# Attention and two MoE layers on one core: the fourth pair's v sums get a buffer of their own and load behind the pair's keys; raw weights load one slot later; slots 6 to 16 and their neighbours get a new order

## The chip, the core and the metric

The kernel runs on one NeuronCore of a Trainium2 chip. The metric is device time in microseconds of one execution, as the median of some executions. Lower is better.

## What is computed

Three layers, one behind the other; all tensors are float32.

```python
# 1. attention, q, k, v: (2, 8, 768, 64); block 32, window 16
k_sum = k.reshape(B, H, 24, 32, D).max(axis=3)      # 24 summary keys per head
v_sum = v.reshape(B, H, 24, 32, D).mean(axis=3)     # 24 summary values per head
scores = softmax over [local keys with |i - j| < 16, 24 summary keys + log(32)]
attn   = a @ [v, v_sum]
# 2. x = attn as (1536, 512);  h = x @ w_in (512, 2048);  g = elu(h);  x2 = g @ w_out
# 3. top-1 mixture of 8 experts on x2: gate by argmax and softmax, relu(x2 @ w1[e]) @ w2[e], times the gate
```

## The kernel before

The 16 heads (2 batches of 8) are taken in pairs, two heads side by side on the 128 partitions. With the 768 tokens of a batch cut into two stretches of 384, there are 16 "pairs" p = 0 to 15: p // 4 is the stretch t, p % 4 the pair of heads. Each pair is done in two units u = 2p and 2p + 1 of three query blocks. The second layer is done in two groups of 8 chunks of the hidden width (f = 0 to 7 and 8 to 15) for each of the four stretches.

The order of all work is written out by hand: one loop over slots, `for sl in range(total)`, and in each slot the instructions are recorded in the order in which every engine and every queue runs them. A slot starts one attention unit (u = sl) while there are any, and from `LAG` = 9 on also a step n = sl - 9 of the second layer.

- Slots 0 to 7 hold attention alone, with small transposes of `busy()` that keep TensorE occupied. In a slot, `pe_s` makes the scores S on TensorE, `dve_max` adds the mask and takes the row minimum on VectorE, `act_exp` is on ScalarE, `norm` scales on VectorE and GpSimd, `pe_t` transposes into T, `act_t` copies T out as pT, `pe_o` multiplies with the values into O, `act_o` copies O out. S, T and O have one PSUM buffer each.
- `prep_k(p + 1)` builds the next pair's key windows `kw` and, for t even, the summary keys. `prep_va(p + 1)` adds up the values of the next pair, read from the tile `vt`, into `va` on VectorE; `pe_va` transposes `va` at the end of the slot, ahead of the next pair's scores; `fin_va` takes the result out as `vs`.
- Loads go through SP's queue, in order. `load_vt(p + 2)` stands in the odd slot of pair p; its tile has one buffer (tag `vt`), so the load waits until `prep_va(p + 1)` has read the buffer.
- The weights of the second layer come as raw 64-bit views: `w_prefetch` loads one raw tile of 512 KB (four buffers), `w_conv` makes float32 of it by three VectorE instructions (lines 396, 400, 403), `w_split` makes the two halves that the fast matmul wants, by a ScalarE cast (L409) and a GpSimd subtraction (L410). In slots 2 to 5 one `w_prefetch` is issued at the end of each.
- Slot 8 is written out by itself: it starts the second layer (`mm1`, line 420) on the first stretch in plain float32. Slots 9 to 16 ("dense") hold one attention unit and one step of the first group; the first stretch uses the converted weights whole, without halves, so splitting (`split_next`) only has to be ready for the second stretch, from slot 17 on.
- `fin` with group 0 takes the sums of a stretch out of PSUM (line 481). `split_x0` makes the two halves of the first stretch's attention output (lines 329, 330); it is not used before the second group, but its buffer is wanted by the last stretch, in slot 26.
- From slot 18 on (p = 9) `pe_s2` starts both units of a pair in an even slot. One of them shares a PSUM buffer with a chunk's hidden values h, so it waits until `elu_max` (line 439) has read h.
- Four converted tiles of the second group are stored to memory early, in slots 23, 27, 29 and 31 (`stash`), and read back later.

The lines that the steps touch: 172 and 173 (`load_vt`), 197 (`prep_k`, the large copy), 481 (`fin`), 899 and 900 (`stash`), 946 to 951 (which weights become ready for splitting in which slot), 1006 to 1011 (start of pair 9), 1092 (`split_x0`), 1181 to 1185 (dense slot), 1202 and 1203 (`load_vt`), 1228 (`w_prefetch`).

Of the kernel before, what the change touches and what calls it, by code (L numbers as in the profile page):

```python
# [9 lines left out]
F32 = mybir.dt.float32  # L10
# [39 lines left out]
def build(tc, cap, qT, kT, vT, vP, wi, wo, wg, wgT, wx, out):  # L50
# [6 lines left out]
    with ctx:  # L57
# [111 lines left out]
        def load_vt(p):  # L169
            t, pr = divmod(p, NPAIR)  # L170
            if t % 2 == 0:
                VT[p] = apool.tile([P, S], F32, tag="vt", bufs=1, name=f"vt{p}")
                nc.sync.dma_start(VT[p], vT[t // 2, pr])

        def load_vw(p):
# [8 lines left out]
        def prep_k(p):  # L184

            t, pr = divmod(p, NPAIR)
            kt = KT[p]
            kw = apool.tile([P, QPT, KEYS], F32, tag="kw", name=f"kw{p}")
            KW[p] = kw
            if t % 2 == 0:  # L190
                KS[p] = apool.tile([P, NSUM], F32, tag=f"ks{pr}", bufs=1, name=f"ks{p}")
                nc.vector.tensor_reduce(
                    out=KS[p], in_=kt[:, WIN : WIN + S].rearrange("p (u s) -> p u s", s=BLK),
                    op=ALU.max, axis=AX.X)
            else:
                KS[p] = KS[p - NPAIR]
            (nc.vector.tensor_copy if p > PB else nc.scalar.copy)(kw[:, :, 0:QB], kt[:, 0:TT].rearrange("p (i k) -> p i k", k=QB))
            rest = nc.gpsimd.tensor_copy if t == 0 and pr else nc.scalar.copy if t == 1 else nc.vector.tensor_copy
            rest(kw[:, :, QB:WK], kt[:, QB : QB + TT].rearrange("p (i k) -> p i k", k=QB)[:, :, 0 : WK - QB])
            (nc.gpsimd if t == 0 and pr else nc.vector).tensor_copy(  # L200
                out=kw[:, :, WK:KEYS], in_=KS[p].unsqueeze(1).to_broadcast([P, QPT, NSUM]))
# [276 lines left out]
        def fin(gr, t, tb):  # L478
            if gr == 0:
                acc[t, tb] = xpool.tile([P, DM], F32, tag=f"a{t}_{tb}", name=f"a{t}_{tb}")  # L480
                nc.scalar.copy(acc[t, tb], accp[tb])
            else:
                a = acc[t, tb]
                nc.vector.tensor_tensor(a, accp[tb], a, op=ALU.add)
                i = t * BPT + tb
                nc.sync.dma_start(x2d[i * P : (i + 1) * P, :], a)
                x2[i] = a
# [408 lines left out]
        nload = [0]  # L896


        stash = [order[2 * FPG + k] for k in (3, 7, 11, 13)]
        S0 = [LAG + 2 * FPG + d for d in (-2, 2, 4, 6)]  # L900
        kept = []

        def w_stash(sl):
# [27 lines left out]
        for sl in range(total):  # L931
# [14 lines left out]
                el = (0, 0, n) if 0 < n < FPG else el if n > FPG else None  # L946
                m2 = (0, 0, n - 1) if 0 <= n - 1 < FPG else None
            cv = list(corder.get(sl, ())) if sl >= LAG else []
            if 0 < n < FPG:
                wpend.append(splits[n - 1])  # L950
            if FPG <= n < FPG + 3:
                wpend.extend(splits[2 * n - FPG - 1 : 2 * n - FPG + 1])
            if FPG + 3 <= n < 2 * FPG - 2:
                wpend.append(splits[n + 2])

            def conv_next():
# [8 lines left out]
            def split_next():  # L965
                if wpend:
                    w_split(*wpend.pop(0))
# [34 lines left out]
            if sl >= 2 * PB:  # L1002
# [3 lines left out]
                if p == PB:  # L1006
                    if even:
                        pe_o(u - 2)
                        act_o(u - 2)
                        dve_o(u - 2)  # L1010
                        fin_va(p)
                        load_vs(p)
                if even and p + 2 < NPR:
# [8 lines left out]
                        load_vw(p + 1)  # L1022
                if el:
                    elu_exp(*el[1:])

                if gr == 1 and nj:
                    rt = t - 1
# [8 lines left out]
                        step(rt)  # L1036
                if el:
                    elu_max(*el[1:])
                    if attn:
                        g_hi(*el[1:])  # L1040
                        g_lo(*el[1:], nc.gpsimd)
# [47 lines left out]
                    blk.first(0, 1)  # L1089
                    conv_expert(0, range(6, 9), pool=range(NCHUNK))  # L1090
                split_next()
                if n in (FPG + 2, FPG + 4):
                    split_x0(n - FPG - 2)
                    split_x0(n - FPG - 1)
                w_stash(sl)
                conv_next()
                if gr == 1 and f % FPG in (3, 4, 5) and t == 3:
# [66 lines left out]
            if u < NU and sl % GPP == 0:  # L1164
                if p + 2 < NPR:
                    load_k(p + 2)
            if u < NU and sl % GPP == 1 and p + 2 < NPR:
                load_q(p + 2)
            if u < NU and sl % GPP == 1 and p and p + 1 < NPR:
# [11 lines left out]
            if dense:  # L1181
                if el:
                    g_hi(*el[1:])
                    g_lo(*el[1:], nc.gpsimd)
                split_next()
                if sl % GPP and p + 1 < NPR:
                    prep_va(p + 1)
                w_conv(cv, (0,))
                if u - 2 in late:
                    dve_o(u - 2)  # L1190
                w_conv(cv, (1,))
                norm(u)
                w_conv(cv, (2,))
                for x in cv:
                    w_prefetch()
                cv = []
            if u < NU and sl % GPP == 0 and p + 1 < NPR:
                prep_k(p + 1)
            if u < NU and sl % GPP == 1 and p + 1 < NPR:
                if not dense:  # L1200
                    prep_va(p + 1)
                if p + 2 < NPR:
                    load_vt(p + 2)
            if sl < LAG and u - 2 in late:
                dve_o(u - 2)
# [19 lines left out]
            if m1:  # L1225
                mm1(*m1[1:])
            conv_next()
            if sl in (LAG - 7, LAG - 6, LAG - 5, LAG - 4):
                w_prefetch()
            if sl < LAG - 1:  # L1230
                busy(2 if sl < LAG - 3 else 4)
# [267 lines left out]
```

## Time and profile before

| | |
|---|---|
| median of 3 runs | 507.85 us (505.27 to 509.25) |
| the profiled execution | 506.81 us |
| its span on the core | 505.0 us |
| TensorE matmul busy | 473.9 us, 94% of the span |
| VectorE, ScalarE, GpSimd busy | 331.8, 266.0, 184.4 us |

The span is what the profile's instructions cover; the execution's own time is 1.8 us longer. TensorE is the engine to watch: a place where it stands still, or where its granted clock is below full, is time that the end can get back. The first 45 us differ from the rest, since attention alone is small work with many hand-overs between engines, and since the transfers of that stretch fill the DMA engines. Idle time of the other engines matters only where TensorE waits behind it.

### The profile page before, as it was taken

To read this page: it belongs to the slowest core of one execution; us is meant where nothing else is said; L and a number is where in the kernel's file an instruction comes from. 1 tells how busy PE (TensorE), PEld (TensorE's weight loads), DVE (VectorE), ACT (ScalarE), POOL (GpSimd) and SP (SyncE) were. 2 spreads that over 40 slices of the span, in tenths; PEclk is the share of its full clock that TensorE was granted. 3 is DMA by queue.
4 is the path that set the end of the run, shared out by engine and by line. 5 is a ranking of instruction groups with operands and counts; after the bars stand their busy time and mean duration, and the time that the engine had idled before them with its cause. 6 is when DMAs were issued, how large, how long until landed. Compare 5 with 4: busy or idle time off the path is not lost. (4 is left out here: it accounts for less than half of the span.)

```text
span 505.0 us, 9045 instructions
## 1 busy us (share of the span) xinstructions
PE 473.9 (94%) x2996; PEld 394.8 (78%) x2996; DVE 331.8 (66%) x886; ACT 266.0 (53%) x667; POOL 184.4 (37%) x189
## 2 busy tenths in 40 slices
PE   6799999889999999999999999999998999999792
PEld 5565555577888889999899899988867989888581
DVE  4566998678656647884259889837686854456560
ACT  4735546676666646565433333344744865466450
POOL 4311443564433326787323333213524030030440
PEclk9979999999999999999999999999999999999998
DMA  8985775324344043449210010013635876376470
GB/s 235 264 234 160 222 240 181 110 79 151 89 144 138 27 167 126 146 126 373 87 62 2 0 62 1 18 46 117 203 115 208 288 241 208 108 225 217 151 247 15
DMA packets 42178, 73.68 MB, mean 146 GB/s; under 512 B 4220, under 2 KB 18812, under 8 KB 42096
## 3 DMA queue, kind: packets, MB, share of 16 engines
q1 hardware_dynamic: 40336, 67.53, 42.5%
q0 software_dynamic: 1760, 5.19, 3.2%
q8 instruction: 34, 0.56, 0.5%
q14 instruction: 48, 0.39, 0.3%
HBM read 62.14 MB, written 9.96 MB: 143 GB/s over the span
## 5 line engine op out<-in xcount | busy, mean ns | idle before, releaser
L427 PE MATMUL h<-xT,Wi 128*128 128x384 f32 x672 | 130.3, 340 | 0.0
L472 PE MATMUL acc<-Wo,g 128*128 128x512 f32 x504 | 126.7, 395 | 0.0
L427 PEld LDWEIGHTS h<-xT,Wi 128*128 128x128 f32 x672 | 118.0, 188 | 5.8 <-issue 1.9
L452 POOL TENSOR_TENSOR g<-e,g 128x384 fp32r<-128x384 f32 x55 | 65.2, 1185 | 132.4 <-ACT g L446 132.4
L472 PEld LDWEIGHTS acc<-Wo,g 128*128 128x128 f32 x504 | 92.9, 188 | 17.4 <-POOL g L452 0.2
L439 DVE SCALAR_TENSOR_TENSOR e<-e,h 128x384 f32<-128x384 f32 x64 | 35.3, 552 | 55.9 <-ACT e L435 53.6
L434 ACT ACTIVATE e<-h 128x384 f32<-128x384 f32 x64 | 31.5, 492 | 58.5 <-PE h L427 55.4
L446 ACT CAST g<-e 128x384 fp32r<-128x384 f32 x56 | 28.8, 514 | 49.2 <-DVE e L439 49.2
L664 DVE TENSOR_TENSOR E<-rawq,E 128x512 fp32r<-128x512 f32 x70 | 47.9, 727 | 7.3 <-ACT E L654 6.0
L796 PE MATMUL bh<-xbq,E 128*128 128x256 f32 (+1 forms) x288 | 43.3, 302 | 2.4 <-issue 1.2
L281 ACT ACTIVATE sc<-sc,st 128x120 f32<-128x120 f32 x96 | 36.7, 385 | 15.8 <-DVE st L274 15.6
L289 POOL TENSOR_TENSOR sc<-sc,st 128x360 f32<-128x360 f32 x32 | 27.4, 857 | 48.2 <-DVE st L288 36.4
L796 PEld LDWEIGHTS bh<-xbq,E 128*128 128x128 f32 x288 | 41.2, 188 | 4.5 <-issue 1.6
L654 ACT CAST E<-rawq 128x512 fp32r<-128x512 f32 x75 | 42.4, 617 | 4.1 <-issue 3.0
L785 PE MATMUL y<-E,g 128*128 128x512 f32 x168 | 41.7, 393 | 0.0
L534 DVE CUSTOM_DVE_ANT_0 dot<-a,wgb 128x512 f32<-128x512 f32 x48 | 40.0, 887 | 0.0
L785 PEld LDWEIGHTS y<-E,g 128*128 128x128 f32 x168 | 30.6, 188 | 5.7
L435 ACT ACTIVATE e<-e 128x384 f32<-128x384 f32 x64 | 33.6, 526 | 2.0
L274 DVE CUSTOM_DVE_ANT_0 sc<-S,masks 128x120 f32<-128x120 f32 x96 | 21.4, 277 | 17.1 <-PE S L249 9.5
L300 ACT COPY pT<-T 120x384 f32<-120x384 f32 x32 | 15.4, 481 | 27.3 <-PE T L296 27.3
L804 DVE TENSOR_TENSOR g<-e,g 128x256 fp32r<-128x256 f32 (+1 forms) x24 | 11.3, 469 | 25.0 <-ACT g L803 24.9
L701 POOL DMA_INDIRECT out<-ys,sidx x6 | 6.3, 1050 | 48.1 <-ACT ys L700 46.6
(248 smaller groups left out, 699.1 us busy)
## 6 DMA issues: line engine op xcount, KB each, us to landing
rawq<-wx SPq DMA_DIRECT2D x88, 256.0 KB, 4.0
rawi<-wi SPq DMA_DIRECT2D x16, 512.0 KB, 7.0
rawo<-wo SPq DMA_DIRECT2D x16, 512.0 KB, 4.3
vw<-vP SPq DMA_DIRECT2D x16, 288.0 KB, 3.3
kt<-kT SPq DMA_DIRECT2D x8, 400.0 KB, 3.4
qt<-qT SPq DMA_DIRECT2D x16, 192.0 KB, 3.1
vt<-vT SPq DMA_DIRECT2D x8, 384.0 KB, 4.2
out<-xg SPq DMA_DIRECT2D x12, 256.0 KB, 4.7
```

The lines of the kernel that those rows point to most:

```text
L281: nc.scalar.activation(out=sc[:, gi], in_=sc[:, gi], func=AF.Exp, bias=st[:, 0, gi : gi + 1], scale=-1.0, accum_out=st[:, 1, gi : gi + 1])
L427: nc.tensor.matmul(HP[t, f][:, 0:TT], lhsT=w[:, s, c * P : (c + 1) * P], rhs=xT[t][:, xs, c, :], start=c == 0 and n == 0, stop=c == NCC - ...
L434: nc.scalar.activation(out=e, in_=HP[t, f][:, 0:TT], func=AF.Exp)
L435: nc.scalar.activation(out=e, in_=e, func=AF.Relu, bias=1.0, scale=-1.0)
L439: nc.vector.scalar_tensor_tensor(out=e, in0=e, scalar=-1.0, in1=h[:, 0:TT], op0=ALU.mult, op1=ALU.max)
L452: eng.tensor_tensor(g[:, 1], EP.pop((t, f)), g[:, 0].bitcast(F32), op=ALU.subtract)
L472: nc.tensor.matmul(accp[tb], lhsT=g[:, s, tb * P : (tb + 1) * P], rhs=w[:, ws], start=f % FPG == 0 and n == 0, stop=f % FPG == FPG - 1 and ...
L534: nc.vector.tensor_tensor_reduce(out=junk, in0=x2[t * BPT + tb], in1=WGB[e // 2][:, e % 2], scale=1.0, scalar=0.0, op0=ALU.mult, op1=ALU.a ...
L654: (nc.vector.tensor_copy if m in vec else nc.scalar.copy)(EW[k][m][:, 0], raw_of(k, m))
L664: (nc.gpsimd if m in pool else nc.vector).tensor_tensor(w[:, 1], raw, w[:, 0].bitcast(F32), op=ALU.subtract)
L785: nc.tensor.matmul(ys[b], lhsT=g[:, s, b * P : (b + 1) * P], rhs=w[:, ws], start=f == 0 and n == 0, stop=f == 7 and n == 2)
L796: nc.tensor.matmul(h[:, 0:nt], lhsT=EW[k][half * NCC + c][:, ws, fc * P : (fc + 1) * P], rhs=xb[:, s, c, 0:nt], start=n == 0, stop=n == 3 ...
```

## The change

1. Pair 3's values are loaded into a tile of their own (space that later holds the stretch 2 activations, tag `xT2`), and the load is issued in the even slot of pair 1, right behind pair 3's keys, not in the odd slot.
2. The four early `w_prefetch` stand in slots 3 to 6, not 2 to 5.
3. Splits: in dense slots 15 and 16 two weights are split, not one; later slots hold correspondingly fewer.
4. `fin` of the first stretch copies on VectorE, not ScalarE. The large copy of `prep_k` for pairs 10 and 11 is on ScalarE, not VectorE.
5. At the start of pair 9 (slot 18) `act_o` and `dve_o` stand later, so `fin_va` is ahead of them.
6. `split_x0` moves from slots 19 and 21 to slots 23 and 25; the stash drops its first tile (three tiles, slots 27, 29, 31), which is then loaded and converted in the second group.

```diff
@@ load_vt
             if t % 2 == 0:
-                VT[p] = apool.tile([P, S], F32, tag="vt", bufs=1, name=f"vt{p}")
+                if p == NPAIR - 1:
+                    VT[p] = xpool.tile([P, NPAIR, S], F32, tag="xT2", name=f"vt{p}")[:, 0]
+                else:
+                    VT[p] = apool.tile([P, S], F32, tag="vt", bufs=1, name=f"vt{p}")
@@ prep_k
-            (nc.vector.tensor_copy if p > PB else nc.scalar.copy)(kw[:, :, 0:QB], ...
+            (nc.vector.tensor_copy if p >= 3 * NPAIR else nc.scalar.copy)(kw[:, :, 0:QB], ...
@@ fin
-                nc.scalar.copy(acc[t, tb], accp[tb])
+                (nc.scalar.copy if t else nc.vector.tensor_copy)(acc[t, tb], accp[tb])
@@
-        stash = [order[2 * FPG + k] for k in (3, 7, 11, 13)]
-        S0 = [LAG + 2 * FPG + d for d in (-2, 2, 4, 6)]
+        stash = [order[2 * FPG + k] for k in (3, 7, 11)]
+        S0 = [LAG + 2 * FPG + d for d in (2, 4, 6)]
@@ which weights become ready for splitting
-            if 0 < n < FPG:
+            if 0 < n < FPG - 2:
                 wpend.append(splits[n - 1])
-            if FPG <= n < FPG + 3:
-                wpend.extend(splits[2 * n - FPG - 1 : 2 * n - FPG + 1])
-            if FPG + 3 <= n < 2 * FPG - 2:
+            if FPG - 2 <= n <= FPG:
+                wpend.extend(splits[2 * n - FPG + 1 : 2 * n - FPG + 3])
+            if FPG < n < 2 * FPG - 2:
                 wpend.append(splits[n + 2])
@@ slot 18
                         pe_o(u - 2)
-                        act_o(u - 2)
-                        dve_o(u - 2)
                         fin_va(p)
...
                 if el:
                     elu_exp(*el[1:])
+                if p == PB and even:
+                    act_o(u - 2)
...
                     elu_max(*el[1:])
+                    if p == PB and even:
+                        dve_o(u - 2)
@@ from slot 18 on
-                if n in (FPG + 2, FPG + 4):
-                    split_x0(n - FPG - 2)
-                    split_x0(n - FPG - 1)
+                if n in (2 * FPG - 2, 2 * FPG):
+                    split_x0(n - 2 * FPG + 2)
+                    split_x0(n - 2 * FPG + 3)
@@ slots up to 17
                     load_k(p + 2)
+                if p + 2 == NPAIR - 1:
+                    load_vt(p + 2)
...
                 split_next()
+                if n >= FPG - 2:
+                    split_next()
...
-                if p + 2 < NPR:
+                if p + 2 < NPR and p + 2 != NPAIR - 1:
                     load_vt(p + 2)
...
-            if sl in (LAG - 7, LAG - 6, LAG - 5, LAG - 4):
+            if sl in (LAG - 6, LAG - 5, LAG - 4, LAG - 3):
                 w_prefetch()
```

SP's queue in slots 2 to 5 (kt keys, qt queries, vt values for the sums, vw values, rawi and rawo raw weights; the digit is the pair or the chunk). Before:

```order
L158 DMA kt3_274<-kT 128x800
L374 DMA rawi0_295<-wi 128x1024
L167 DMA qt3_323<-qT 128x384
L180 DMA vw2_325<-vP 96x6x128
L173 DMA vt3_337<-vT 128x768
L374 DMA rawi1_342<-wi 128x1024
L225 DMA vw2_325<-vs2_372 24x6x128
L160 DMA kt4_375<-kT 128x416
L374 DMA rawi2_395<-wi 128x1024
```

The same place of SP's queue in the changed kernel (its own line numbers):

```order
L158 DMA kt3_274<-kT 128x800
L176 DMA vt3_276<-vT 128x768
L167 DMA qt3_323<-qT 128x384
L183 DMA vw2_325<-vP 96x6x128
L377 DMA rawi0_340<-wi 128x1024
L228 DMA vw2_325<-vs2_370 24x6x128
L160 DMA kt4_373<-kT 128x416
L377 DMA rawi1_393<-wi 128x1024
L167 DMA qt4_421<-qT 128x384
L183 DMA vw3_423<-vP 96x6x128
L377 DMA rawi2_438<-wi 128x1024
```

vt3 moved from fourth place behind kt3 to the first, and each raw tile moved behind the attention loads of the next slot.

GpSimd in slots 15 to 17 (sc are attention weights being scaled, Wi and Wo the low halves of split weights). Before, and then in the changed kernel:

```order
L410 TENSOR_TENSOR Wo1_1025<-T4_495,Wo1_1025 128x512
L289 TENSOR_TENSOR sc15_1015<-sc15_1015,st15_1016 128x360
L410 TENSOR_TENSOR Wi4_1081<-T6_496,Wi4_1081 128x512
L289 TENSOR_TENSOR sc16_1071<-sc16_1071,st16_1072 128x360
L410 TENSOR_TENSOR Wo2_1120<-T6_496,Wo2_1120 128x512
L289 TENSOR_TENSOR sc17_1127<-sc17_1127,st17_1128 128x360
```

```order
L413 TENSOR_TENSOR Wo1_1025<-T4_493,Wo1_1025 128x512
L413 TENSOR_TENSOR Wi4_1028<-T6_494,Wi4_1028 128x512
L292 TENSOR_TENSOR sc15_1015<-sc15_1015,st15_1016 128x360
L413 TENSOR_TENSOR Wo2_1084<-T6_494,Wo2_1084 128x512
L413 TENSOR_TENSOR Wi5_1087<-T8_495,Wi5_1087 128x512
L292 TENSOR_TENSOR sc16_1074<-sc16_1074,st16_1075 128x360
L413 TENSOR_TENSOR Wo3_1126<-T8_495,Wo3_1126 128x512
```

Two subtractions now stand back to back in slots 15 and 16.

ScalarE from slot 17 into slot 18 (a is the stretch's sum, e and g the ELU of chunk 8). Before, and then in the changed kernel:

```order
L323 CAST xT1_705<-O15_1113 128x192
L481 COPY a0_0_1146<-acc0_0_0_728 128x512
L481 COPY a0_1_1148<-acc0_0_1_729 128x512
L481 COPY a0_2_1150<-acc0_0_2_730 128x512
L409 CAST Wi5_1152<-T8_497 128x512
L300 COPY pT16_1174<-T16_1168 120x384
L323 CAST xT2_1183<-O16_1176 128x192
L220 ACTIVATE vs9_1186<-T16_1168 24x128
L434 ACTIVATE e1_0_1191<-h1_0_1155 128x384
L435 ACTIVATE e1_0_1191<-e1_0_1191 128x384
```

```order
L326 CAST xT1_705<-O15_1119 128x192
L412 CAST Wi6_1158<-T10_496 128x512
L303 COPY pT16_1180<-T16_1174 120x384
L223 ACTIVATE vs9_1189<-T16_1174 24x128
L437 ACTIVATE e1_0_1194<-h1_0_1161 128x384
L438 ACTIVATE e1_0_1194<-e1_0_1194 128x384
L326 CAST xT2_1197<-O16_1182 128x192
```

The three copies of a left this engine (they stand on VectorE, ahead of `elu_max` of chunk 8), and pT16, vs9 and the two steps of e moved forward.

## Rows read from the trace of the kernel before

**Rows 1.** Stretches: start:end, length, each engine's busy us (instructions), clock, DMA, GB/s.

```profile
25.00:30.00 5.00, 4.04 (x31) 3.07 (x32) 2.38 (x13) 1.76 (x9) 0.79 (x1) 0.56 1.09 271
30.00:35.00 5.00, 5.00 (x50) 4.05 (x50) 3.34 (x12) 2.88 (x12) 0.79 (x1) 0.75 0.80 221
220.00:230.00 10.00, 10.00 (x53) 9.21 (x52) 7.09 (x8) 6.66 (x14) 7.71 (x8) 1.00 0.74 244
```

**Rows 2.** Timeline: start, us, engine, line, instruction [idle before <-releaser], slots 5 to 8.

```profile
24.95 0.95 DVE L206 TENSOR_REDUCE va<-vt 128x24 f32<-128x768 f32 x1 [2.88 <-DMA vt<-vT]
...
25.96 0.47 PE L214 MATMUL V<-ident,va 128*120 128x128 f32 x1 [2.89 <-DVE va L206]
...
26.36 1.47 PE L260 MATMUL S<-kw,qt 64*64 64x120 f32 x12
...
31.33 1.37 PE L260 MATMUL S<-kw,qt 64*64 64x120 f32 x12
...
34.63 0.83 PE L260 MATMUL S<-kw,qt 64*64 64x120 f32 x12
```

**Rows 3.** Timeline, the same matmuls one pair earlier, in slots 4 and 5, and two small transposes.

```profile
18.06 0.83 PE L260 MATMUL S<-kw,qt 64*64 64x120 f32 x12
...
18.82 0.44 PE L864 MATMUL warm<-ident 128*128 128x128 f32 x2
...
20.38 0.83 PE L260 MATMUL S<-kw,qt 64*64 64x120 f32 x12
```

**Rows 4.** Timeline: arrivals and conversions of raw weights in slots 2 to 8.

```profile
19.65 0.35 POOL L199 COPY kw<-kt 128x192 f32<-128x192 f32 x1 [0.52 <-DMA kt<-kT]
...
29.88 0.40 DVE L396 TENSOR_SCALAR T<-rawi 128x512 uint32<-128x512 uint32 x1
...
31.51 0.69 DVE L403 SCALAR_TENSOR_TENSOR T<-rawi,T 128x512 uint32<-128x512 uint32 x1
...
36.99 0.42 DVE L396 TENSOR_SCALAR T<-rawi 128x512 uint32<-128x512 uint32 x1
...
42.91 0.83 PE L260 MATMUL S<-kw,qt 64*64 64x120 f32 x12
```

**Rows 5.** DMA from 8 to 34 us.

```profile
DMA packets 4531, 6.46 MB, mean 249 GB/s; under 512 B 329, under 2 KB 3357, under 8 KB 4526
```

**Rows 6.** Timeline, slots 14 to 16: GpSimd's subtractions beside VectorE, and TensorE's waits.

```profile
85.58 1.27 POOL L410 TENSOR_TENSOR Wo<-T,Wo 128x512 fp32r<-128x512 f32 x1 [3.72 <-ACT Wo L409]
85.64 1.75 DVE L400 SCALAR_TENSOR_TENSOR x<-rawo,x 128x512 uint32<-128x512 uint32 x1
...
88.31 2.84 PE L468 MATMUL acc<-x,e 128*128 128x512 f32 x6 [0.41 <-DVE x L403]
...
90.25 0.68 DVE L400 SCALAR_TENSOR_TENSOR x<-rawo,x 128x512 uint32<-128x512 uint32 x1
90.54 1.52 POOL L410 TENSOR_TENSOR Wi<-T,Wi 128x512 fp32r<-128x512 f32 x1 [1.63 <-ACT Wi L409]
```

**Rows 7.** Timeline, slots 17 to 22: TensorE's waits and what stands ahead of them.

```profile
96.59 1.55 ACT L481 COPY a<-acc 128x512 f32<-128x512 f32 x3
...
99.09 0.57 PE L308 MATMUL O<-pT,vw 120*64 120x64 f32 x12 [0.79 <-ACT pT L300]
...
100.42 0.52 PE L296 MATMUL T<-ident,sc 128*120 128x128 f32 x3 [0.76 <-POOL Wi L410]
...
102.03 0.83 PE L249 MATMUL S<-kw,qt 64*64 64x120 f32 x20 [0.74 <-DVE e L439]
...
113.38 0.92 PE L351 MATMUL O<-pT,vw 120*64 120x64 f32 x24 [0.63 <-DVE xT L337]
...
115.56 0.83 PE L249 MATMUL S<-kw,qt 64*64 64x120 f32 x20 [0.91 <-DVE e L439]
...
127.62 0.83 PE L249 MATMUL S<-kw,qt 64*64 64x120 f32 x20 [0.70 <-DVE e L439]
```

**Rows 8.** Timeline, VectorE at the end of slot 25.

```profile
148.12 0.55 DVE L439 SCALAR_TENSOR_TENSOR e<-e,h 128x384 f32<-128x384 f32 x1 [2.48 <-ACT e L435]
```

More of the change, by code (lines that the diff above doesn't have):

```diff
@@ L196, in prep_k @@
                 KS[p] = KS[p - NPAIR]
-            (nc.vector.tensor_copy if p > PB else nc.scalar.copy)(kw[:, :, 0:QB], kt[:, 0:TT].rearrange("p (i k) -> p i k", k=QB))
+            (nc.vector.tensor_copy if p >= 3 * NPAIR else nc.scalar.copy)(kw[:, :, 0:QB], kt[:, 0:TT].rearrange("p (i k) -> p i k", k=QB))
             rest = nc.gpsimd.tensor_copy if t == 0 and pr else nc.scalar.copy if t == 1 else nc.vector.tensor_copy
```

## The prediction

> **What bounds the kernel now.** I read first where TensorE stands still or runs below its full clock, because in most of the span it does neither: in a stretch such as 220 to 230 us it is busy for 10.00 of 10 us at a granted clock of 1.00, while VectorE has 7.09 [rows 1]. In such a stretch only less TensorE work would help. The change takes away no TensorE instruction, so its gain must come from the holes.
>
> The largest hole is in the prologue, at the end of slot 5. VectorE waits 2.88 us for the values of the fourth pair (vt3), whose sum it can start only at 24.95; TensorE, which transposes that sum next, waits 2.89 us until 25.96 [rows 2]. The price is higher than the wait. The granted clock is 0.56 in the stretch from 25 to 30 us and 0.75 from 30 to 35 [rows 1], that is, TensorE spends most of them at the lower of its two levels, 1.2 and not 2.4 GHz: the twelve matmuls of a unit's scores take 1.47 and 1.37 us in slots 6 and 7, and 0.83 in slots 4, 5 and 8 [rows 2, 3]. What it did before the fall was to stand still for those 2.89 us.
>
> The smaller holes lie in slots 15 to 22. TensorE waits 0.41 us for the conversion of a weight [rows 6]; in slots 17 and 18 it waits 0.79, 0.76 and 0.74 us for ScalarE and what hangs on it; in slots 20 and 22 it waits 0.63, 0.91 and 0.70 us for VectorE [rows 7]. From there to past 330 us I found no wait of TensorE worth naming; nothing later is tied to an absolute time, so what is saved before should reach the end.
>
> **Step 1, the prologue.** Before, vt3 stood fourth behind kt3 in SP's queue, with 992 KB (rawi0, qt3, vw2) between them, and waited for its buffer; now it is right behind kt3 and waits for no buffer. The DMA engines move 249 GB/s on the mean from 8 to 34 us [rows 5], so I take them as full and the transfers as served in order. kt3 has landed by 19.65 [rows 4]; 384 KB more take 1.6 us, so vt3 is there by about 21.2. VectorE would reach its sum at 24.95 - 2.88 = 22.07. The wait goes, with 0.9 us to spare, and TensorE starts pair 3 at 23.1 in place of 25.96.
>
> How much of the clock comes back is read from the same code one pair earlier. From the scores of slot 4 to those of slot 5 it is 2.32 us [rows 3]; slots 6 and 7 each hold four more small transposes (two take 0.44 us with their start [rows 3], so four more about 0.4), and took 4.97 and 3.30 us [rows 2]. At full clock that would be 2.7 each, so 2.9 us less in all. Not all of it arrives: VectorE converts the first raw weight in slot 6 (the three instructions take about 2.3 us, from 29.88 on [rows 4]), so the row minima of slot 7 start some 0.3 us later than TensorE would allow, and slot 8's scores need the same PSUM buffer. I take 2.5. With 2.9 for the wait, slot 8 starts 5.4 us earlier. Bounds: 2.9 if the clock falls anyway, 5.8 if nothing holds it back.
>
> What is late next? Every raw tile is issued later, but its need also comes 5.4 us earlier. The five transfers from kt3 to rawi0 are those that before went from kt3 to vt3, in another order, so rawi0 lands when vt3 did, at 24.95. It is needed 3.5 us after slot 6's scores [rows 2, 4], of which 0.6 is the slow clock, so at 26.2: 1.2 us to spare. rawi1 has 792 KB more ahead of it and in it, 3.3 us, so it lands at 28.2 and is needed in slot 7, about 30.3. rawi2 has another 992 KB, 4.1 us: 32.3, and VectorE wants it at about 32.6, where before it was 36.99 [rows 4]. That is the tightest, but TensorE uses the result only after slot 9's scores at 42.91 - 5.4 = 37.5, so a delay of up to 3 us there should stay hidden behind slot 8's matmuls. In the queue itself nothing that attention needs moves back: qt3, vw2, kt4, qt4 and vw3 all have fewer bytes ahead of them.
>
> **Step 2, two splits in slots 15 and 16.** Each slot gets a ScalarE cast and one more GpSimd subtraction of 1.27 to 1.52 us. VectorE pays for it: its second conversion step took 1.75 us while GpSimd subtracted, and 0.68 us where it started before GpSimd [rows 6]. So one more subtraction costs VectorE about 1.07 us, and in these two slots VectorE is what TensorE waits for: the sum over chunk 6 already waits 0.41 us for a converted weight [rows 6]. I charge 1.1 us for each slot, +2.2. Bounds: nothing, if the subtraction falls beside work that it doesn't hold up, and 2 x 1.52 = +3.0 if VectorE stands for all of it. The Trainium skill (SBUF — State Buffer, section "SBUF: two separate sides") says that VectorE with two SBUF inputs, or in a two-port mode, and GpSimd share one pair of ports as an exclusive lock, held for the whole instruction, the loser blocked. By that rule two subtractions back to back cost up to two whole ones, which is the +3.0; the 1.75 us row agrees with a block, but it lost 1.07 and not 1.27, since it could come in late.
>
> **Step 3, slots 17 and 18.** Three copies of 1.55 us together leave ScalarE just ahead of pT16, and vs9 and the two steps of the ELU no longer stand behind a copy that needs TensorE's next result. The three waits of 0.79, 0.76 and 0.74 us hang on that chain [rows 7]. The copies go to VectorE, ahead of the ELU's maximum, for which TensorE's scores wait; if they start after slot 16's delay, they end close to when the maximum is wanted. I take -1.4 of the 2.29; bounds -2.3 and 0.
>
> **Step 4, slots 19 to 22.** In slots 19 and 21 VectorE loses a large copy of the keys (ScalarE takes it in the place of a cast that moved forward) and the eight instructions of `split_x0`. These stood ahead of the waits of 0.63, 0.91 and 0.70 us [rows 7]. The surplus is larger than the waits, so I take all of it, -2.2; the other bound is -0.7, if the shift of the subtractions on GpSimd keeps VectorE late in slot 19.
>
> **Step 5, what lands elsewhere.** `split_x0` in slot 23 takes the place of a conversion of about the same length that moved out; in slot 25 VectorE waits 2.48 us at the end of the slot [rows 8], enough for four instructions of less than 0.6 each. The dropped stash tile costs one conversion in the second group, where VectorE has 2.9 of 10 us free and TensorE is full [rows 1]. I take 0; if the cover is gone in both slots, it is twice the 0.70 that the same code cost in slot 22 [rows 7], +1.4.
>
> **The sum.** -5.4 + 2.2 - 1.4 - 2.2 + 0 = -6.8 us. The profiled execution took 506.81 us, so 500.0. The median of the runs is 1.04 us higher; taken from that it would be 501.0. I say 500.5.
>
> **The rivals.**
>
> Only the wait goes, the clock does not come back, or vt3 still comes late: step 1 gives -2.9 or less. For it: small pauses remain in slots 5 to 8. Against: slots 4 and 5 have the same pauses at full clock [rows 3]. -2.9 - 1.4 = -4.3, so 502.5 to 503.5.
>
> The new order eats part of the gain: GpSimd's subtractions in slots 15 and 16 cost the upper bound, and the copies of a on VectorE delay the maximum, so step 2 is +3.0 and step 3 is 0, and step 4 gives only -0.7. For it: VectorE is already what TensorE waits for there [rows 6]. -5.4 + 2.3 = -3.1: 503.7 to 504.8. The lock rule of the Trainium skill, taken at its word, is this case.
>
> The holes close fully and the subtractions are hidden: -5.8 - 2.3 - 2.2 = -10.3: 496.5 to 498.
>
> The other side, slower: the stall moves from vt3 to rawi2. If it lands after about 36, TensorE stands still in slot 8 or 9 and the clock falls again, now in front of the float32 matmuls. From slot 8's scores to slot 9's is 42.91 - 34.63 = 8.3 us at full clock [rows 2, 4]; at half it costs up to 8.3 more. Less the 5.4 and 1.4 that stay, +1.5 beside the wait itself: 508 to 512. It decides at a landing some 3.5 us later than worked out; against it speaks that no more bytes are ahead of it than were ahead of rawo0 before.
>
> **How the numbers follow.** Forecast 0.62, with its own range 498.3 to 502.7; only the wait 0.10; the order eats the gain 0.15; all holes close 0.08; slower 0.05. The range 497.0 to 504.7 leaves out the slower case and parts of the two beside it, about 0.14. Faster by over 1% means below 502.8, and 1% is about what a measurement of this kernel can tell from no change: 0.58 of the forecast, 0.08 and a little of the others, 0.68. Within 1%: 0.27. Slower: 0.05.
>
> **What would show it.** Step 1: no wait of VectorE for vt, a granted clock of 1.00 from 25 to 35 us, 0.83 us for the scores of slots 6 and 7, and slot 9's scores at about 37.5. A wait of VectorE for rawi in slots 6 to 8 would show the weights as the new stall. Step 2: the sums over chunks 6 and 7 wait for a converted weight by 1 to 2 us. Steps 3 and 4: the waits of slots 17 to 22 gone or below 0.3 us each. Step 5: no wait of TensorE in slots 23 to 27. The forecast is wrong if slot 9 starts later than 39.5, or if the lead there is not found again at slot 30.

## The result, and the profile after

The changed kernel takes 502.38 us (median of 6 runs, 500.68 to 502.5); the kernel before, beside it on the same chip, 508.2 us (504.85 to 510.24). The ratio is 0.989, with a 95% interval of 0.986 to 0.992: faster, by 1.1%. The forecast was 500.5 with a range of 497.0 to 504.7. The profiled execution has a span of 500.6 us, against 505.0.

TensorE runs the same matmuls in the same order in both kernels, and in all those below, apart from the idle transposes. So the start of one matmul can be compared between two traces; I call the difference the **lead** (negative: earlier than in the kernel before). What a stage costs is how the lead changes over it.

Stretches of the kernel after: start:end, length, busy us (instructions) of TensorE, its weight load, VectorE, ScalarE and GpSimd, then the granted clock, the DMA share and GB/s.

```profile
8.00:14.00 6.00, 5.41 (x39) 3.90 (x39) 3.75 (x18) 3.48 (x15) 1.45 (x3) 0.72 0.80 209
25.00:30.00 5.00, 4.45 (x60) 3.46 (x57) 3.69 (x17) 2.80 (x12) 1.18 (x2) 1.00 1.03 268
30.00:35.00 5.00, 5.00 (x42) 3.29 (x40) 3.92 (x12) 2.40 (x10) 0.79 (x1) 1.00 1.05 312
465.00:470.00 5.00, 5.00 (x16) 3.91 (x15) 1.65 (x4) 2.29 (x5) 0.96 (x1) 0.66 0.25 69
```

The clock from 25 to 35 us is 1.00, where it was 0.56 and 0.75 [rows 1]. But it is 0.72 from 8 to 14 us, ahead of everything that the change touches (before: 1.00), and 0.66 in the tail.

The timeline of the kernel after (start, us, engine, line, instruction, idle before and what ended it), in the order of time: the start, slots 5 to 9, slots 15 to 18, slots 20 and 22, and the second group.

```profile
8.05 0.33 PE L217 MATMUL V<-ident,va 128*120 128x128 f32 x1 [1.95 <-DVE va L209]
8.31 1.46 PE L263 MATMUL S<-kw,qt 64*64 64x120 f32 x12
10.75 1.28 PE L263 MATMUL S<-kw,qt 64*64 64x120 f32 x12
...
23.20 0.95 DVE L209 TENSOR_REDUCE va<-vt 128x24 f32<-128x768 f32 x1
24.46 0.83 PE L263 MATMUL S<-kw,qt 64*64 64x120 f32 x12
26.42 0.57 PE L311 MATMUL O<-pT,vw 120*64 120x64 f32 x12 [0.55 <-DMA vw<-vs]
27.84 0.83 PE L263 MATMUL S<-kw,qt 64*64 64x120 f32 x12
38.88 0.83 PE L263 MATMUL S<-kw,qt 64*64 64x120 f32 x12
...
85.37 2.84 PE L471 MATMUL acc<-x,e 128*128 128x512 f32 x6 [1.48 <-DVE x L406]
90.95 2.84 PE L471 MATMUL acc<-x,e 128*128 128x512 f32 x6 [1.15 <-DVE x L406]
96.90 0.57 PE L311 MATMUL O<-pT,vw 120*64 120x64 f32 x12 [0.57 <-ACT pT L303]
98.85 0.83 PE L252 MATMUL S<-kw,qt 64*64 64x120 f32 x20 [0.56 <-DVE e L442]
...
110.37 0.84 PE L252 MATMUL S<-kw,qt 64*64 64x120 f32 x24
121.48 0.85 PE L252 MATMUL S<-kw,qt 64*64 64x120 f32 x24
...
232.22 0.68 DVE L399 TENSOR_SCALAR t1o<-rawo 128x512 uint32<-128x512 uint32 x1 [1.25 <-DMA rawo<-wo]
237.49 1.89 PE L475 MATMUL acc<-Wo,g 128*128 128x512 f32 x7 [0.24 <-POOL g L455]
```

The fourth pair's sum at 23.20 waits for nothing, where VectorE waited 2.88 us [rows 2], and the scores of slots 6 and 7 take 0.83 us in place of 1.47 and 1.37. Slot 9's scores start at 38.88 and not at 42.91 [rows 4]: a lead of -4.03, although the first slots lost 1.08 us at the low clock. The sums over chunks 6 and 7, which need the weights that slots 15 and 16 convert, wait 1.48 and 1.15 us. Slots 17 and 18 still wait 0.57 and 0.56; the waits of slots 20 and 22 are gone, and their scores run as one group of 24. At 237 us there is a small new wait.

The table gives the change of the lead over each stage, in us, for every kernel run here, worked out from the starts of the same matmuls. "Start" reaches to slot 5's scores, "5 to 8" from there to slot 9's. Up to 350 us the stages left out change the lead of no kernel by more than 0.02 us. Behind 350 us it changes by +1.29 us in the kernel after and by anything from -1.73 (a_start_busy) to +3.05 (e_split_x0) in the others; what sets that stretch was not looked into by a run of its own.

| kernel | start | 5 to 8 | 15, 16 | 17, 18 | 19 to 24 | near 237 us |
|---|---|---|---|---|---|---|
| after | +1.08 | -5.11 | +2.05 | -1.20 | -2.96 | +0.49 |
| e_prologue_only | +2.15 | -5.34 | 0 | 0 | 0 | +0.18 |
| e_order_only | +0.92 | -1.16 | +2.04 | -1.19 | -2.97 | +0.48 |
| e_cover | +3.71 | -3.87 | 0 | 0 | 0 | 0 |
| e_place_only | -0.32 | -1.63 | 0 | +2.79 | -1.33 | +0.18 |
| a_start_busy | +0.62 | -3.76 | +2.04 | -1.20 | -2.97 | +0.49 |
| e_one_split | +1.12 | -5.33 | 0 | -1.19 | -2.69 | +0.75 |
| e_fin_act | +1.28 | -5.33 | +2.05 | -0.99 | -2.96 | +0.48 |
| e_slot18 | -0.33 | -5.33 | +2.05 | -0.22 | -2.98 | +0.48 |
| e_x0_keys | +1.24 | -3.43 | +2.05 | -1.20 | -1.71 | +0.51 |
| e_split_x0 | -0.73 | -4.57 | 0 | -1.20 | 0 | +0.48 |
| e_stash4 | +0.56 | -4.31 | +2.05 | -1.20 | -2.90 | +0.18 |
| a_best | -0.44 | -4.57 | 0 | -1.20 | -1.74 | 0 |

Where two kernels share the edits of a stage, the columns from slot 15 on agree to some hundredths, e_place_only apart, so one profile settles what an edit does there. e_place_only and the six kernels from e_one_split to e_stash4 ran once each (e_fin_act 501.65 us, e_slot18 501.63, e_x0_keys 504.12, e_split_x0 503.64, e_stash4 501.51), so for them the traces decide and not the times. The first two columns don't repeat, and that turned out to be the larger lesson.

### The profile page after: what moved, and what is told of

Its sections match the earlier page's. It is cut to its first block, busy times and chain, and to the rows that moved or that the text cites. A ratio compares the mean times of both kernels' runs of the same rounds, so it can differ in the third digit from the quotient of the medians.

```text
span 500.6 us, 9042 instructions
## 1 busy us (share of the span) xinstructions
PE 473.9 (95%) x2996; PEld 394.3 (79%) x2996; DVE 336.2 (67%) x887; ACT 265.3 (53%) x666; POOL 184.4 (37%) x189
```

## The experiments

**The two halves of the change.** The kernel before with step 1 alone:

```
+ own tile for vt3, loaded behind kt3        (as in the change)
- if sl in (LAG - 7, LAG - 6, LAG - 5, LAG - 4):
+ if sl in (LAG - 6, LAG - 5, LAG - 4, LAG - 3):
      w_prefetch()
```

> The kernel before with step 1 alone: the own place for vt3, its load behind kt3, and the raw weights one slot later; the order of slots 6 to 16 and all that follows stay as before. Theory (step 1 is worth the wait and the clock): no wait for vt at the fourth pair, granted clock 1.00 from 25 to 35 us, slot 9's scores 5.1 to 5.4 us earlier than in the kernel before once a later or earlier start of the first slots is taken off, and the time 5 us lower, about 0.990 of before. Rival (the gain in the time comes mostly from the new order, and what the prologue wins is waited away in slots 15 to 22, where the transfers or VectorE set the pace): slot 9 earlier by 5, but the lead shrinks to 2 or 3 us by slot 22 and the time is 0.995 or above.

It took 504.08 us against 507.58; ratio 0.9935 (0.9905 to 0.9965). In the profile slots 5 to 8 gained 5.34 us and the lead stayed to the last slot of attention, as the theory says. But the medians fell by 3.5, not by 5: the interval leaves out the theory's 0.990 by little and holds the rival's 0.995, while the lead that stays rules out the rival's reason. I come back to it.

The kernel after with those lines as before, so the new order alone:

> The kernel after with step 1 undone: vt3 in the old buffer and at its old place in the queue, raw weights loaded at the old slots; only the new order remains. Theory: the wait for vt3 and the low clock from 25 to 35 us are back; by slot 22 TensorE leads the kernel before by 1.4 to 2.1 us (2.05 lost in slots 15 and 16, about 1.2 and 3.0 gained in slots 17, 18 and in 19 to 22), time 0.996 to 0.998 of before. Rival (the waits of slots 17 to 22 only vanished because the prologue ran 5 us earlier, against loads that did not move): the waits of slots 17 to 22 stay, the two splits still cost 2 us, and the time is 1.00 to 1.004.

505.38 us against 507.58; ratio 0.9984 (0.9952 to 1.0016). Stage by stage the order does exactly what it does in the kernel after, +2.04, -1.19 and -2.97, so its gains don't hang on the earlier prologue: the rival falls. In time it is a gain too small for these runs to tell from none. The two medians, 3.5 and 2.2 us lower, add to 5.7, near the 5.8 of the whole change; the two ratios add to 0.8% and not 1.1%, so the agreement is no closer than their intervals.

**The two halves of step 1.** The kernel before with vt3's place and early load, and the raw weights loaded at their old slots:

> The kernel before with vt3 in its own place and loaded behind kt3, and the raw weights at their old slots; nothing else. Theory (the order of the transfers decides, and rawi0 now stands between vt3 and the queries and values of the next pairs): vt3's wait goes as in the kernel after, but TensorE waits in slot 6 for the vs of pair 2 by about 2 us (512 KB of rawi1 ahead of it at 249 GB/s) more than the 0.55 us of the kernel after, so slot 9 leads the kernel before, start taken off, by about 3 and not 5.1 us. Rival (the raw loads' place does not matter, the DMA engines had room): slot 9 leads by 5.

Its timeline, TensorE in slots 6, 7, 9 and 18:

```profile
26.94 0.57 PE L311 MATMUL O<-pT,vw 120*64 120x64 f32 x12 [2.22 <-DMA vw<-vs]
28.90 1.47 PE L263 MATMUL S<-kw,qt 64*64 64x120 f32 x12
40.95 0.83 PE L263 MATMUL S<-kw,qt 64*64 64x120 f32 x12
97.14 0.57 PE L311 MATMUL O<-pT,vw 120*64 120x64 f32 x12 [0.78 <-ACT pT L303]
98.46 0.51 PE L299 MATMUL T<-ident,sc 128*120 128x128 f32 x3 [0.76 <-POOL Wi L413]
98.90 0.42 PE L252 MATMUL S<-kw,qt 64*64 64x120 f32 x4
100.07 1.47 PE L252 MATMUL S<-kw,qt 64*64 64x120 f32 x20 [0.74 <-DVE e L442]
101.47 4.21 PE L430 MATMUL h<-xT,Wi 128*128 128x384 f32 x12
```

The wait for vt3 is gone, and TensorE waits 2.22 us for the vs of pair 2 in place of it; the clock falls behind this wait as it did behind the other, and the scores of slot 7 take 1.47 us. Slots 5 to 8 gain 1.63 us and not 5.1. So **the later raw loads carry 3.5 of step 1's 5.1 us** in this pair of profiles; against all nine kernels that have both halves (-3.43 to -5.34) it is 1.8 to 3.7, and 3.7 against e_slot18, which started alike. The gain of 1.63 is less than the 3 expected, which did not count a fall of the clock. The one execution took 508.3 us. In slot 18 the waits are those of the kernel before, 0.79, 0.76 and 0.74 [rows 7]; there the scores behind them took 0.83 us, and here 1.47, with the next matmuls at the low clock as well. The same pauses cost this execution 2.79 us more; 1.33 of them come back at slots 20 and 22, where less is left to wait for. What vt3's own tile and its place in the queue are worth apart was not run. Before, its load was issued at 17.77 us, just when the sum of pair 2 (from 16.80, 0.95 us long) had released the buffer; in the kernel after it was issued at 15.93, ahead of that sum (17.88), so the early place needs the tile.

**What the clock costs.** The kernel before with `if sl == 5: busy(16)` ahead of the fourth pair's v sums:

> The kernel before with 16 more idle transposes (as those at the start, 0.19 us each there) on TensorE at the end of slot 5, ahead of the fourth pair's v sums, so that TensorE is busy while it waits for vt3; the wait of VectorE for vt3 stays. Theory (the low clock from 25 to 35 us follows from TensorE's standing still for 2.89 us, and costs 2.5 us): VectorE waits 2.9 us as before, but the clock is 1.00 in that stretch, the scores of slots 6 and 7 take 0.83 us, slot 9's scores come 2.2 to 2.5 us earlier, and the time is about 0.995. Rival (what the clock gives back is waited for elsewhere, on VectorE and the raw weights): the scores of slots 6 and 7 take 0.83 us, but slot 9 comes less than 1 us earlier and the time is 0.998 to 1.00.

506.49 us; ratio 0.9994 (0.9959 to 1.0029). It doesn't answer its question. The timeline around the place, VectorE and TensorE:

```profile
25.83 0.95 DVE L206 TENSOR_REDUCE va<-vt 128x24 f32<-128x768 f32 x1
26.61 1.91 PE L864 MATMUL warm<-ident 128*128 128x128 f32 x16
28.36 0.27 PE L214 MATMUL V<-ident,va 128*120 128x128 f32 x1
28.56 0.83 PE L260 MATMUL S<-kw,qt 64*64 64x120 f32 x12
```

In this execution the first slots were 3.71 us late, so vt3 was there in time, VectorE waited for nothing, and the 16 transposes were in the way rather than a cover. Slot 9 came at 42.75 all the same: **a late start and the wait for vt3 don't add up, the one hides the other.** The rival's numbers came out (0.83 us, slot 9 earlier by 0.16, a ratio of 0.9994), but not for its reason.

Still, the run prices the clock. From slot 6's scores to slot 9's it takes 14.19 us, in the order of before and at a granted clock of 1.00 from 25 to 35 us; the kernel before takes 16.55 [rows 2, 4]. In e_order_only it is 15.29 (slot 9 at 42.67):

```profile
27.12 0.33 PE L214 MATMUL V<-ident,va 128*120 128x128 f32 x1 [3.12 <-DVE va L206]
27.38 1.24 PE L260 MATMUL S<-kw,qt 64*64 64x120 f32 x12
```

There slot 7's scores took 0.83 us again. So the fall of the clock cost about 1.1 us in this execution and 2.4 in that of the kernel before, an estimate from these three profiles, behind waits of 3.12 and 2.89 us. The kernel after takes 14.42 in the same stretch, with its wait for vs.

**The start.** The kernel after with `busy(32)` in place of `busy(24)`:

> The kernel after with 32 instead of 24 idle transposes at the start, so that TensorE stands still for some 0.5 us and not for 1.95 us ahead of the first pair's sums. Theory (the low clock of slots 0 and 1 in the profile of the kernel after, where the scores took 1.46 and 1.28 us, follows from that pause, and comes in most executions): the scores of slots 0 and 1 take 0.83 us, slot 9 starts about 1 us earlier than in the kernel after, time about 1 us under that of the kernel after, 0.987 of before. Rival (the profile caught a rare late first transfer; most executions have no low clock there): the time is that of the kernel after within 0.3 us; more idle transposes than the wait holds would make it later instead by up to 0.5 us.

500.4 us; ratio 0.9896 (0.9852 to 0.9939). From the timeline, TensorE in slots 0, 1 and 6:

```profile
8.46 0.33 PE L217 MATMUL V<-ident,va 128*120 128x128 f32 x1 [0.87 <-DVE va L209]
8.71 0.83 PE L263 MATMUL S<-kw,qt 64*64 64x120 f32 x12
10.44 0.83 PE L263 MATMUL S<-kw,qt 64*64 64x120 f32 x12 [0.30 <-DVE st L277]
27.31 0.57 PE L311 MATMUL O<-pT,vw 120*64 120x64 f32 x12 [1.07 <-DMA vw<-vs]
```

The first sum was available later than in the kernel after (V at 8.46, not 8.05), and yet the clock didn't fall, so slot 1 began earlier (10.44, not 10.75). The 0.3 us and more were then given back: TensorE waits 1.07 us for vs in slot 6. The ratio can't be told from that of the kernel after. Of the theory the clock holds in the trace (0.83 us in slots 0 and 1), but slot 9 did not come 1 us earlier: it came at 39.77, 0.89 later than in the profile of the kernel after. For the time neither is decided.

**Step 2.** The kernel after with one split in slots 15 and 16:

```
- if n >= FPG - 2:
-     split_next()
  (and two pieces handed on in slots 17 to 19, as before)
```

> The kernel after with one split in slots 15 and 16 again (and so two in each of slots 17 to 19 as before); all else stays. Theory (the 2.05 us lost in slots 15 and 16 are the second subtraction on GpSimd, beside which VectorE's conversion runs slower; and slots 17, 18 gain because casts have left ScalarE there): the sums over chunks 6 and 7 wait 0.4 and 0.2 us as in the kernel before, slots 15 and 16 get their 2.05 us back, but slots 17 and 18 lose their 1.2 us again, and slots 19 to 22 some of their 3.0. Rival (the gains of slots 17 to 22 come from the copies and from split_x0 alone): the 2.05 us come back and nothing is lost later; the kernel is then 2 us faster than the kernel after.

```profile
84.11 2.84 PE L471 MATMUL acc<-x,e 128*128 128x512 f32 x6 [0.40 <-DVE x L406]
88.73 2.84 PE L471 MATMUL acc<-x,e 128*128 128x512 f32 x6 [0.19 <-DVE x L406]
94.68 0.57 PE L311 MATMUL O<-pT,vw 120*64 120x64 f32 x12 [0.57 <-ACT pT L303]
96.63 0.83 PE L252 MATMUL S<-kw,qt 64*64 64x120 f32 x20 [0.56 <-DVE e L442]
```

The waits of chunks 6 and 7 are back at 0.40 and 0.19, nothing is lost in slots 17 and 18, and 0.3 at slot 20. Near 237 us another 0.26 is lost. The rival has it in the main: **this edit costs more than it gives**, 2.05 us there for 0.3 at slot 20. The one execution took 500.51 us.

GpSimd's second subtraction and VectorE beside it, in slots 15 and 16 of the kernel after:

```profile
82.78 1.72 POOL L413 TENSOR_TENSOR Wi<-T,Wi 128x512 fp32r<-128x512 f32 x1
83.29 1.23 DVE L290 TENSOR_SCALAR st<-st 128x3 f32<-128x3 f32 x1
...
89.07 1.27 POOL L413 TENSOR_TENSOR Wi<-T,Wi 128x512 fp32r<-128x512 f32 x1
89.27 1.63 DVE L406 SCALAR_TENSOR_TENSOR x<-rawo,x 128x512 uint32<-128x512 uint32 x1
```

In e_one_split, without that subtraction, the same two VectorE instructions take 0.16 us (at 83.11) and 0.66 (at 88.01). The differences of 1.07 and 0.97 are the stage's 2.05. In slot 15 it isn't the conversion that is held up but the small scaling ahead of its last step.

**Step 3**, in two parts. The copies of the accumulators on ScalarE again (`nc.scalar.copy(acc[t, tb], accp[tb])`):

> The kernel after with the three copies of the first accumulators on ScalarE again and not on VectorE; the new place of the steps of attention in slot 18 and all else stay. Theory (step 3 hangs on these three copies of 1.55 us together, which stand ahead of what TensorE waits for on ScalarE): TensorE's waits of slots 17 and 18 come back, 1.2 us or more are lost between slots 16 and 19 against the kernel after. Rival (the moved steps in slot 18 and the casts that left slots 17 to 19 bring it): less than 0.4 us is lost.

Only 0.21 us is lost; the wait for pT in slot 17 goes from 0.57 to 0.79. Then the other part, slot 16's `act_o` and `dve_o` back ahead of the ELU in slot 18:

> The kernel after with the steps of attention in slot 18 at their old place: the copies of slot 16's unit stand ahead of the two steps of the ELU on ScalarE and VectorE again, and not behind them. The three copies of the accumulators stay on VectorE. Theory, after the run with these copies back on ScalarE lost only 0.21 us: the other 0.99 us of step 3 are the moved steps, so TensorE waits again in slot 18 and 0.99 us are lost against the kernel after between slots 17 and 19. Rival (neither part alone matters, since either alone takes enough off ScalarE): less than 0.3 us is lost.

```profile
95.26 0.57 PE L311 MATMUL O<-pT,vw 120*64 120x64 f32 x12 [0.57 <-ACT pT L303]
96.58 0.52 PE L299 MATMUL T<-ident,sc 128*120 128x128 f32 x3 [0.76 <-issue]
98.19 0.83 PE L252 MATMUL S<-kw,qt 64*64 64x120 f32 x20 [0.74 <-DVE e L442]
```

0.98 us is lost, the waits of 0.76 and 0.74 are back, and the 0.57 stays. The moved steps carry step 3, and the copies 0.2 of it; the two add to the whole 1.20.

**Step 4.** The kernel after with `split_x0` in slots 19 and 21 and the copies of the keys on VectorE again:

> The kernel after with step 4's work back on VectorE: the eight instructions of split_x0 in slots 19 and 21, and the large copy of the keys of the two pairs concerned on VectorE and not on ScalarE. Theory (step 4 hangs on that work): the waits of slots 20 and 22 come back, at least the 2.2 us of the three waits shown of before are lost between slots 19 and 22 against the kernel after. Rival (the slots got free because the splits are spread otherwise, so that conversions start earlier): less than 1 us is lost.

TensorE's scores of slot 20 there:

```profile
112.24 1.10 PE L252 MATMUL S<-kw,qt 64*64 64x120 f32 x24
```

Slot 22 loses its 1.15 us again, with a wait of 0.70 ahead of 20 of its scores. Slot 20 loses only 0.25 of its 2.0, and 0.14 of that comes back right behind it. So I undid e_one_split's part as well:

> The kernel after with both undone that alone cost little in slot 20: one split in slots 15 and 16 (so two in slots 17 to 19), and split_x0 and the copies of the keys back on VectorE in slots 19 and 21. Measured against the kernel after: the one alone gained 2.05 us in slots 15 and 16 and lost 0.32 at slot 20; the other alone lost 0.25 at slot 20 and 1.15 at slot 22. Theory (slot 19 holds too much work for VectorE and GpSimd only when both are in it; either removal is enough): both together lose 2.0 us at slot 20, as the kernel before does, and 1.1 at slot 22. Rival (the two are independent): 0.6 us at slot 20 and 1.1 at slot 22.

```profile
106.87 0.92 PE L354 MATMUL O<-pT,vw 120*64 120x64 f32 x24 [0.63 <-DVE xT L340]
109.05 0.83 PE L252 MATMUL S<-kw,qt 64*64 64x120 f32 x20 [0.91 <-DVE e L442]
121.12 0.83 PE L252 MATMUL S<-kw,qt 64*64 64x120 f32 x20 [0.70 <-DVE e L442]
```

All three waits are back at the lengths of [rows 7], and 2.00 us are lost at slot 20. Slot 19 holds too much only with both in it; taking out either one is enough but for 0.3 us. The effects don't add.

**The wait near 237 us.** Four tiles set aside in the first group, as before:

> The kernel after with four converted tiles set aside in the first group again, not three. Theory (the 0.49 us that the kernel after loses near 237 us, in a wait for GpSimd's result behind a raw output weight that VectorE waits for, follows from the dropped fourth tile, which must be loaded raw and converted again in the second group, behind twelve writes in SP's queue): the 0.49 us vanish, and slot 13 or 14 pays for the fourth tile, at most 0.5 us. Rival (the loss follows from the 5 us earlier arrival at a load whose place in the queue did not move): the 0.49 us stay.

0.31 of the 0.49 us come back there and 0.06 are paid in slot 24. The other 0.18 are lost in e_prologue_only and e_place_only too, which have the four tiles, but not in a_best, which has them as well and the largest lead; so they don't come from the lead alone, and their cause stays open. The theory is right for two thirds of the loss.

**A combination.** One split in slots 15 and 16, `busy(32)`, the first raw weight's load right behind the vs of pair 2, four tiles set aside, and the splits from slot 17 on spread as two, two and then one each up to slot 23:

> The kernel after with four edits that the runs so far speak for: one split in slots 15 and 16, two in slots 17 and 18, one each after that; 32 idle transposes at the start; the first raw weight's load right behind the vs of pair 2 in SP's queue, and not ahead of it; four tiles set aside again. Theory: slots 15 and 16 gain 2.05 us, slot 19 does not lose the 0.3 us that two splits cost there, TensorE's wait for vs in slot 6 (0.55 us in the kernel after, 1.07 us with 32 transposes) goes below 0.3 us, 0.3 us come back near 237 us; together 2.5 to 4 us less than the kernel after, 0.980 to 0.984 of before. Rival (the first raw weight is then late for VectorE in slot 6, and the minima of slot 7 with it, so that TensorE waits there instead): slots 6 to 8 lose 1 us or more and the time is 0.984 to 0.987.

499.77 us against 506.39 (6 and 11 runs); ratio 0.9864 (0.9812 to 0.9917), less than expected. The wait for vs is gone, slots 5 to 8 gain 0.8 us more than with the 32 transposes alone (0.5 less than in the profile of the kernel after: TensorE waits 0.27 us for qt and 0.52 in slot 8), and slots 15 and 16 have their 2 us, but slot 24 has a new wait. VectorE and TensorE there:

```profile
125.10 1.26 DVE L333 TENSOR_TENSOR xT<-x,xT 128x384 fp32r<-128x384 f32 x1
126.29 1.44 DVE L332 CAST xT<-x 128x384 fp32r<-128x384 f32 x1
...
130.63 0.83 PE L252 MATMUL S<-kw,qt 64*64 64x120 f32 x20 [0.78 <-DVE e L442]
```

My spread put one more split into the slot that now holds `split_x0`. Its second cast takes 1.44 us beside that split's subtraction on GpSimd, where it takes 0.35 in the kernel after (the 1.26 stands there too, as 1.25), and 1.2 us are lost. It beats the kernel before clearly; that it beats the kernel after is not shown, since the intervals overlap. An estimate from the 1.2 here and the 0.3 of e_one_split: with that kernel's own spread and the other three edits it would be about 0.9 us better still; it wasn't run.

## Why the prediction was right, and where it was off

**The sum.** -6.8 was forecast. Net of the start, the lead behind slot 22 is -7.2; with it -6.14. At the end of the trace 4.4 remain: +1.08 was lost at the start, 0.49 near 237 us, and 1.3 behind 350 us, in waits and at the low clock of the tail (0.66 from 465 to 470 us), a stretch that gave up to 1.73 and took up to 3.05 in the other profiles. The prediction had held that what is saved before would reach the end; in one profile that is not to be seen. The medians differ by 5.8.

**Step 1 (-5.4).** The mechanism is as forecast: no wait for vt, full clock, 0.83 us for the scores, no wait of VectorE for a raw weight. In the profile it is -5.11: from slot 5's scores to slot 6's 3.00 us and not 5.98, which is 2.98 for the 2.9 of the wait, and from there to slot 9's 14.42 and not 16.55, which is 2.13 for the 2.5 of the clock. The forecast of slot 9 at 37.5 failed (38.88), and the failing step is "what is late next": it followed the raw weights and held that nothing attention needs moves back in the queue. That was true and not enough, since the need for the vs of pair 2 comes about 3 us earlier while one raw load of 512 KB less (2.1 us at the 249 GB/s of [rows 5]) stands ahead of it. It is waited for by 0.55 us here and by 0.96, 1.07 and 1.11 in e_stash4, a_start_busy and e_x0_keys. It is waited for as long in e_split_x0 (1.08), by 0.32 in e_fin_act, and not at all in e_prologue_only, e_one_split and e_slot18, with the same loads. More weighs that one profile stood for all: in the nine kernels with step 1 and its order of loads slot 9's scores start from 37.25 to 40.73, mean 38.97, and in three of them behind the 39.5 at which the prediction would have called itself wrong; in before, e_order_only and e_cover at 42.91, 42.67 and 42.75. The mean gain is thus about 3.8 us, near the 3.5 that e_prologue_only measured; the profile of that kernel, with 5.34 in slots 5 to 8, had lost 2.15 at the start. So step 1 is worth some 1.6 less than the 5.4, and that is most of the 1.9 by which the forecast was too low; this is worked out from one profile a kernel and not shown by the times. e_place_only shows that the slower rival's kind of event, a stall moved to another transfer with the clock falling again, was close by: in that profile only the later raw loads would have kept it out.

**Step 2 (+2.2): +2.05**, right in size and mechanism, and undone by e_one_split. The +3.0 of two whole subtractions did not come. The Trainium skill's rule (SBUF — State Buffer, section "SBUF: two separate sides") is that, of GpSimd and a VectorE instruction with two SBUF inputs or in a two-port mode, whichever starts first has the shared ports for its whole instruction and the other fully blocks. The trace agrees with it: the VectorE scaling that began at 83.29 ended at 84.52, and the subtraction that began at 82.78 ended at 84.50 (in which mode the scaling runs, the trace doesn't say). What I made of the rule was too much, since VectorE came 0.51 and 0.20 us behind the start of the subtractions and paid only for what was left.

**Step 3 (-1.4): -1.20**, right in size. I gave it to the three copies and to the steps moved behind the ELU together, with the copies named first; the copies are worth 0.2 and the moved steps 1.0. The sign that I set, waits below 0.3 us, failed here: 0.57 and 0.56 are left in slots 17 and 18.

**Step 4 (-2.2): -2.96**, mis-sized beyond its own bound. The three waits add to 2.24. The rest is that TensorE's group of scores is no longer broken: 24 matmuls in one go take 0.84 us (110.37 above), while 4 and 20 apart, as in e_place_only's slot 18 above (there at the low clock for the 20) or in [rows 7] for the 20 alone, take 0.42 and 0.83. Twice 0.41 is about the 0.7 that is missing. And I named the cause too simply: at slot 20 either of two edits is enough. I had counted the other one, the shift of the subtractions, only as a risk.

**Step 5 (0).** No wait in slots 23 to 27, as forecast. The dropped tile costs 0.31 us near 237, where I had taken it as free since TensorE is full there.

## What to carry to other kernels

When a late transfer is taken off the path, look for the next one by what moves its need as well as by the bytes ahead of it, and count every transfer of the stage, the small ones too. Undo each edit of a bundle alone: here one edit cost 2 us and gave back 0.3 to 0.5, another had most of a gain that I had not divided, and two hid each other. Before a prologue's gain is taken from one trace, see how far its start differs between executions.

## What was not expected of the hardware

The first slots run the same instructions in twelve of these kernels (all but the two with `busy(32)`), and yet slot 5's scores start between 19.65 and 24.09 us. Part is the landing of the first values: VectorE's first sum starts from 5.79 to 7.61 us. Part is the clock. Over all fourteen profiles, where TensorE stood still for 1.47 us or less ahead of the first pair's sums, slot 0's scores took 0.83 us (ten times). With 1.95, 2.13 and 2.54 us they took 1.46 or 1.47. At 1.48 us slot 0 took 0.83 and slot 1 1.47, in e_one_split:

```profile
8.56 0.33 PE L217 MATMUL V<-ident,va 128*120 128x128 f32 x1 [1.48 <-DVE va L209]
8.82 0.83 PE L263 MATMUL S<-kw,qt 64*64 64x120 f32 x12
10.54 1.47 PE L263 MATMUL S<-kw,qt 64*64 64x120 f32 x12 [0.31 <-DVE st L277]
```

Shorter pauses were followed by the low clock too. In e_cover TensorE stood still for 0.72, 1.03 and 0.88 us in slots 1 and 2, and slot 3's scores took 1.47 us. Pauses of under 0.8 us each, three in a row, left the clock alone in slot 18 of the kernel before and of e_prologue_only and were followed by the low one in e_place_only. So a small wait has a price that is not its length, in some executions only. Whether the removal of such waits is why the runs of the kernel after lie closer together (1.8 us, before 5.4) is not shown: these are six runs each, and in twelve runs each e_prologue_only, whose prologue is the same, spreads by 5.8 and e_order_only by 6.3.
